# ScalarE's exponentials placed ahead of the sinks' copy and of the values' copy in an attention kernel with a written-out order

## The chip, the cores and the metric

One core of a Trainium2 chip runs one program. The core has five engines with a queue each, worked in order: TensorE (PE in the profile; its weight loads are PEld), VectorE (DVE), ScalarE (ACT), GpSimd (POOL) and SyncE (SP, which here issues the DMAs). An engine waits on semaphores for what the others produce. Times are device microseconds (us) of one execution; the metric is the median over runs.

## The reference

Two parts, one after the other. Attention for batch 4, 8 heads, 768 positions, head size 64: each query sees the first 4 keys (the sinks) and the 128 latest keys up to itself. Then a mixing layer and a feed-forward layer on the 512 columns that the heads make together:

```python
keep = is_sink | in_window                     # n_sink = 4, window = 128
scores = np.where(keep, scale * q @ k.T, -1e9)
a = np.exp(scores - np.max(scores, axis=-1, keepdims=True))
x = (a / (np.sum(a, axis=-1, keepdims=True) + 1e-09)) @ v
...
u = x + np.real(np.fft.fft(np.fft.fft(x, axis=1), axis=2))
un = (u - mean(u)) / np.sqrt(var(u) + 1e-06)
out = u + np.maximum(un @ w_ch1, 0.0) @ w_ch2  # 512 -> 2048 -> 512
```

All is float32.

## The kernel before

**Blocks and steps.** The attention goes over 24 blocks: 4 batches of 6 blocks of 128 queries. A block has 4 steps, one for each pair of heads. So step s works on block g = s // 4 and pair s % 4, called here the first to the fourth step of a block (k = 0 to 3). Every operation of a pair or a block is issued a fixed number of steps after its scores: `STEP_LAG` for what is done per pair, `BLOCK_AT` for what is done per block. A step therefore holds the scores of one pair, the exponentials of the pair two steps earlier, the transposes of an earlier one, and so on.

**One pair, in order.** PE makes the scores (L700, L702) in a PSUM tile `s`, of which there are two. DVE merges the older key block into the place of the masked newer keys (`merge`, L708) and subtracts the maximum with the mask (`soft1`, L720) into the tile `sm`. ACT takes the exponentials of the two heads, one ACTIVATE each, with their sums (`expo`, L726, two steps after the scores). POOL copies the sinks' four columns aside as a rounded part and a remainder (`sink_p`, L737 and L738). PE transposes the probabilities of four heads (`trans_p`, L751), ACT copies them out of PSUM (`copy_p`, L758, tile `pta`), POOL splits them into newer and older keys (L767, L775), and PE multiplies by the values (`av`, L789) into `xt`.

**One block.** PE transposes the sinks' probabilities (`trans_sink`, L809); the result lies in a part of the score tile of the second pair two blocks later, so the merge into that tile comes after ACT has copied it out (`copy_sink`, L814, tile `skt`, always in a block's second step). ACT copies the values' product `xt` out of PSUM (`copy_x`, L794, tile `xs`, always in a fourth step). PE turns it and adds the sinks' part (`turn_x`, L801, L803), and DVE scales it into the residual (`store_x`, L819).

**The Fourier mix** of a batch starts when its blocks are stored, and runs as events between the steps of the next batch: folds on DVE and POOL (L351, L358, L361), a rounded copy on ACT (`gh`, L364) and its remainder on DVE (`gl`, L367), products on PE (L394, L421, L442), their copies on ACT (L399, L401, L425, L430) and remainders or sums on DVE (L406, L409, L447, L448), updates on POOL (L458, L459). On ACT these copies are the entry `"A"` of an order. They free the PSUM bank that PE's next product takes.

**What sets the order.** In steps 0 to 96 each engine's instructions are issued exactly in the order that the table `SCHEDULE` writes out: a row for each of the four steps of a block, for each of the four engines A (ACT), V (DVE), G (POOL), T (PE). The table has two sets of rows: the first for steps below `PHASE = 36`, the second from there on. An entry with nothing to do in a step (as `sink_hi` outside the first step, or `copy_p` in the first and third) issues nothing. From step `CUT = 97` on the framework's planner places the instructions, by costs that it assumes, up to the end of the first group of the feed-forward layer. The weights' conversions (`convert`, L590 to L592 on DVE, L607 on ACT, L608 on POOL) belong to it. Then come the other groups of the feed-forward layer (L619, L1124 on PE), again in written order.

Of the kernel before, what the change touches and what calls it, by code (L numbers as in the profile page):

```python
# [83 lines left out]
    {  # L84
        "A": [
            ["copy_x", "copy_p", "copy_sink", "expo", "A", "sink_hi"],
            ["copy_x", "copy_sink", "expo", "sink_hi", "A", "copy_p"],
            ["copy_x", "copy_p", "copy_sink", "expo", "A", "sink_hi"],
            ["copy_x", "A", "copy_p", "copy_sink", "expo", "sink_hi"],
        ],  # L90
        "V": [
            ["inverse", "store_x", "sink_lo", "V", 3, 0, 1, 2, "merge", "soft1"],
# [17 lines left out]
    {  # L110
        "A": [
            ["copy_x", "copy_p", "A", "sink_hi", "copy_sink", "expo"],
            ["copy_x", "copy_sink", "A", "sink_hi", "copy_p", "expo"],
            ["copy_x", "copy_p", "copy_sink", "expo", "A", "sink_hi"],
            ["expo", "copy_x", "copy_p", "copy_sink", "A", "sink_hi"],
        ],
# [1220 lines left out]
```

## Time and profile before

| | us |
|---|---|
| median of 3 runs | 787.84 (786.68 to 789.1) |
| the profiled execution | 786.78 |
| its span | 784.9 |
| PE busy in it | 755.2 |
| DVE busy | 460.6 |
| ACT busy | 239.0 |
| POOL busy | 177.6 |
| last exponential of the attention starts | 205.5 |

The profile gives for each group of instructions the line, the engine, the operation, the tiles (out<-in), their number and time, and the idle time of the engine just ahead of them with the instruction that ended it. In a listing in order of time, the columns are start, duration, engine, line, operation, tiles, shapes and count; idle time stands in brackets behind.

### The profile page before, as it was taken

Reading aid. Unit: us, or ns where it says so; the run is one execution under the profiler, and the core shown is the slowest. Engines: PE = TensorE matmul, PEld = TensorE weight load, DVE = VectorE, ACT = ScalarE, POOL = GpSimd, SP = SyncE. Lnnn points to the kernel's source line nnn. Section 1 sums busy time; section 2 is a strip of 40 time slices with the busy share of each in tenths; the row PEclk is TensorE's granted clock in tenths of the full one; section 3 lists DMA queues with packets and bytes.
Section 4 is the critical chain, followed back from the end, with each engine's and each line's share of the span. In section 5 each row is a group of like instructions: output and inputs, shape, how many; then the busy total and the mean of one; then the engine's idle time right before and its main releaser. Section 6 shows DMA issues by size and latency. Waiting matters only on the chain.

```text
span 784.9 us, 11953 instructions
## 1 busy us (share of the span) xinstructions
PE 755.2 (96%) x4379; PEld 615.8 (78%) x4379; DVE 460.6 (59%) x1354; ACT 239.0 (30%) x704; POOL 177.6 (23%) x283
## 2 busy tenths in 40 slices
PE   7999998988899999999999999999999999999996
PEld 5666876866778878899888888888888888888895
DVE  6788687999999589561356424662456425611211
ACT  4887765756633133221111111111111110110110
POOL 2566477476645255200000000000000000000000
PEclk9999999999999999999999999999999999999999
DMA  9853525433305366120100002000200001000100
GB/s 311 251 171 109 140 84 176 127 112 99 131 27 159 111 196 210 62 71 1 54 1 0 1 9 99 1 1 0 81 1 0 1 0 54 1 1 0 55 1 32
DMA packets 41812, 57.69 MB, mean 74 GB/s; under 512 B 2796, under 2 KB 27500, under 8 KB 41360
## 3 DMA queue, kind: packets, MB, share of 16 engines
q1 hardware_dynamic: 41456, 53.07, 21.7%
q0 software_dynamic: 288, 3.76, 1.2%
q8 instruction: 37, 0.61, 0.3%
q14 instruction: 31, 0.25, 0.1%
HBM read 47.37 MB, written 9.45 MB: 72 GB/s over the span
## 4 chain that ended last, share of the span: by engine, by line
PE 80%; DVE 13%; issue 2%; POOL 1%; ACT 1%; DMA 1%; SPq 0%; DVEq 0%; ACTq 0%; POOLq 0%
PE h L619 33%; PE o L1124 33%; PE xt L789 3%; PE s L702 3%; DVE sm L720 2%; PE pt L751 2%; DVE cv L591 1%; PE za L394 1%; DVE s L708 1%; DVE cv L590 1%; PE a L421 1%; DVE cv L592 1%; DVE f L351 1%; PE x L801 1%; DMA vt<-in_v_sink_dram 1%
## 5 line engine op out<-in xcount | busy, mean ns | idle before, releaser
L1124 PE MATMUL o<-w,h 128*128 128x512 f32 x876 | 216.5, 394 | 0.0
L1117 DVE SCALAR_TENSOR_TENSOR h<-h,h 128x512 fp32r<-128x512 f32 (+1 forms) x107 | 65.4, 611 | 247.7 <-ACT h L1112 247.5
L1124 PEld LDWEIGHTS o<-w,h 128*128 128x128 f32 x876 | 162.8, 188 | 35.5
L1112 ACT ACTIVATE h<-h 128x512 fp32r<-128x512 f32 (+1 forms) x107 | 57.2, 535 | 366.4 <-PE h L619 360.1
L619 PE MATMUL h<-un_slots,w 128*128 128x512 f32 (+1 forms) x576 | 124.7, 365 | 0.0
L619 PEld LDWEIGHTS h<-un_slots,w 128*128 128x128 f32 x576 | 99.6, 188 | 19.6
L619 PE MATMUL h<-un_last,w 128*128 128x512 f32 (+1 forms) x432 | 89.0, 355 | 0.0
L619 PEld LDWEIGHTS h<-un_last,w 128*128 128x128 f32 x432 | 72.7, 188 | 12.8
L726 ACT ACTIVATE sm<-sm,mx 128x132 f32<-128x132 f32 x192 | 75.8, 400 | 7.1 <-DVE mx L720 7.1
L1148 DVE STREAM_TRANSPOSE unf<-un 32x128 f32<-32x128 f32 x224 | 67.7, 302 | 3.2
L702 PE MATMUL s<-ring,q 64*128 64x260 f32 x320 | 51.2, 422 | 12.2 <-DVE mx L720 6.4
L720 DVE CUSTOM_DVE_ANT_0 sm<-s,mask 128x132 f32<-128x132 f32 x192 | 48.7, 292 | 9.3 <-ACT skt L814 2.7
L702 PEld LDWEIGHTS s<-ring,q 64*128 64x128 f32 x320 | 27.1, 188 | 28.2 <-issue 12.4
L608 POOL TENSOR_TENSOR w<-cv,w 128x512 fp32r<-128x512 f32 x25 | 33.9, 1354 | 35.5 <-ACT w L607 35.4
L789 PE MATMUL xt<-ptl,ldv 128*64 128x128 f32 x384 | 38.9, 288 | 0.0
L708 DVE COPY_PREDICATED s<-older,s 128x256 f32<-128x256 uint8 x80 | 33.6, 420 | 7.2 <-ACT skt L814 6.8
L726 ACT ACTIVATION_READ_ACCUMULATOR sm<-sm,mx 128x1 f32 x192 | 36.8, 192 | 0.0
L1124 PE MATMUL o<-w_ring,h 128*128 128x512 f32 x144 | 35.6, 393 | 0.0
L767 POOL TENSOR_SCALAR_AFFINE_SELECT ptl<-pta 128x512 f32<-128x512 f32 x48 | 32.2, 672 | 14.4 <-ACT pta L758 14.4
L789 PEld LDWEIGHTS xt<-ptl,ldv 128*64 128x64 f32 x384 | 21.6, 137 | 14.9 <-issue 8.1
L789 PE MATMUL xt<-pta,ldv 128*64 128x128 f32 x320 | 31.7, 277 | 0.2 <-POOL pta L775 0.2
L751 PE MATMUL pt<-ident,sm 128*128 128x128 f32 x192 | 31.6, 288 | 0.0
(200 smaller groups left out, 1040.9 us busy)
## 6 DMA issues: line engine op xcount, KB each, us to landing
raw<-in_moe_w_ch_dram SPq DMA_DIRECT2D x32, 512.0 KB, 3.7
ldv<-in_v_dram SPq DMA_DIRECT2D x28, 256.0 KB, 3.6
ring<-in_qk_dram SPq DMA_DIRECT2D x24, 264.0 KB, 4.6
out_dram<-u SPq DMA_DIRECT2D x24, 256.0 KB, 3.8
q<-in_qk_dram SPq DMA_DIRECT2D x20, 256.0 KB, 4.2
cst<-in_dft_dram POOLq DMA_DIRECT2D x1, 3348.0 KB, 11.7
ud<-us SPq DMA_DIRECT2D x12, 256.0 KB, 2.2
u<-ud SPq DMA_DIRECT2D x2, 1024.0 KB, 5.1
```

What stands on the lines that cost most here:

```text
L608: G.tensor_tensor(d[1], tf, f32(d[0]), op=ALU.subtract)
L619: T.matmul(ps[:, :tb], a[:, cs], x[:, :, cc, :], start=n == 0, stop=n == 3 * NCC - 1)
L702: T.matmul(ps[:, j, :P + W], st["q", g][rows, hp, :], keys(g, 2 * hp + j), start=True, stop=True)
L708: V.copy_predicated(ps[:, :, P + NS:P + W], older[qi > 2], ps[:, :, 0:P])
L720: V.tensor_tensor_reduce(sm[:, h % 4], ps[:, j, P:P + W], mask[min(qi, 3)], -SCALE, 3.0e38, ALU.add, ALU.min, accum_out=mx[:, 0, h:h + 1])
L726: A.activation(sm[:, h % 4], sm[:, h % 4], AF.Exp, bias=mx[:, 0, h:h + 1], scale=-1.0, accum_out=mx[:, 1, h:h + 1])
L751: T.transpose(ps[:, j], sm[:, j, NS:], ident)
L789: T.matmul(ps[D * j:D * j + D, p, :], st["v", kb(g) - i][:, h, :], a[:, h % 4, :], start=i == 0, stop=i == n - 1)
L1112: A.activation(h[0], ps[:, :tb], AF.Relu)
L1117: V.scalar_tensor_tensor(h[1], ps[:, :tb], 0.0, f32(h[0]), op0=ALU.max, op1=ALU.subtract)
L1124: T.matmul(po[i], a[:, ts_], x, start=f == 0 and n == 0, stop=f == NF - 1 and n == 2)
L1148: V.transpose(unf[32 * q:32 * q + 32, :, r], un[r].rearrange("p (c q j) -> p c q j", c=NCC, q=4)[:, :, q])
```

## The change

Three rows of the order of ACT are written differently; no instruction is added or taken away.

```diff
 SCHEDULE = [
     {
         "A": [
             ["copy_x", "copy_p", "copy_sink", "expo", "A", "sink_hi"],
-            ["copy_x", "copy_sink", "expo", "sink_hi", "A", "copy_p"],
+            ["copy_x", "expo", "copy_sink", "copy_p", "A", "sink_hi"],
             ["copy_x", "copy_p", "copy_sink", "expo", "A", "sink_hi"],
-            ["copy_x", "A", "copy_p", "copy_sink", "expo", "sink_hi"],
+            ["expo", "copy_x", "A", "copy_p", "copy_sink", "sink_hi"],
         ],
...
     {
         "A": [
             ["copy_x", "copy_p", "A", "sink_hi", "copy_sink", "expo"],
-            ["copy_x", "copy_sink", "A", "sink_hi", "copy_p", "expo"],
+            ["copy_x", "expo", "copy_sink", "copy_p", "A", "sink_hi"],
             ["copy_x", "copy_p", "copy_sink", "expo", "A", "sink_hi"],
             ["expo", "copy_x", "copy_p", "copy_sink", "A", "sink_hi"],
         ],
```

In the second step of a block the exponentials go ahead of the sinks' copy, in both sets of rows, and the Fourier copies (`"A"`) go behind the probabilities' copy. In the fourth step of the first set the exponentials go ahead of the values' copy; the second set had that order already. The second step's exponentials are those of the fourth pair of the block before; the fourth step's are those of the second pair of its own block.

## The prediction

> **What bounds the kernel now.** I read the page first, then busy time by stretch, then the groups of instructions, last the single queues in order of time.
>
> ```profile
> PE 755.2 (96%) x4379; PEld 615.8 (78%) x4379; DVE 460.6 (59%) x1354; ACT 239.0 (30%) x704; POOL 177.6 (23%) x283
> ```
>
> ScalarE (ACT), the only engine whose order is edited, is busy 30% of the span. The edited steps end near 208 us, so what counts is that part, by stretch (columns: length, then busy time with the count of instructions of PE, weight loads, DVE, ACT, POOL, then the granted clock, DMA share, GB/s):
>
> ```profile
> 17.00:57.00 40.00, 39.14 (x374) 27.62 (x375) 32.40 (x167) 32.98 (x132) 22.18 (x51) 0.97 0.73 233
> 57.00:72.00 15.00, 13.17 (x118) 8.67 (x117) 13.89 (x58) 11.35 (x45) 12.53 (x22) 1.00 0.36 110
> 72.00:105.00 33.00, 33.00 (x297) 27.65 (x296) 21.59 (x94) 22.46 (x84) 15.19 (x33) 1.00 0.42 114
> 105.00:122.00 17.00, 13.01 (x108) 9.12 (x107) 15.73 (x48) 11.30 (x43) 14.11 (x22) 0.98 0.28 80
> 159.00:186.00 27.00, 20.95 (x180) 15.48 (x180) 26.45 (x84) 15.74 (x54) 20.85 (x34) 1.00 0.38 113
> 200.00:256.00 56.00, 52.14 (x324) 44.31 (x321) 55.51 (x96) 22.34 (x52) 32.44 (x30) 0.97 0.32 102
> ```
>
> Two kinds alternate. In 17 to 57 and 72 to 105 us PE has 0.86 and 0 us idle: it is the bound, and a wait moved on ACT, DVE or POOL changes nothing. In 57 to 72, 105 to 122, 159 to 186 and 200 to 256 us DVE is 93 to 99% busy and PE idles 1.8, 4.0, 6.1 and 3.9 us. There only what shortens DVE's own queue helps. ACT binds no stretch.
>
> Who waits around the edit, from the groups (after the bar: busy us and mean ns of one, then idle time before and its releasers):
>
> ```profile
> L726 ACT ACTIVATE sm<-sm,mx 128x132 f32<-128x132 f32 x192 | 75.8, 400 | 7.1 <-DVE mx L720 7.1
> L708 DVE COPY_PREDICATED s<-older,s 128x256 f32<-128x256 uint8 x80 | 33.6, 420 | 7.2 <-ACT skt L814 6.8 <-PE s L702 0.5
> L794 ACT COPY xs<-xt 128x512 f32<-128x512 f32 x24 | 14.1, 586 | 16.7 <-PE xt L789 16.2 <-PE x L801 0.5
> L737 POOL CAST sk<-sm 128x32 fp32r<-128x32 f32 x48 | 11.3, 236 | 58.9 <-ACT sm L726 58.7
> ```
>
> The exponentials wait only 7.1 us for their input, so they can mostly run where they are put; behind one that did wait would stand skt and pta, and behind skt DVE's merge. The values' copy (xs) waits 16.2 us for PE. POOL loses 58.7 us waiting for exponentials. And DVE's merge waits 6.8 us for the sinks' copy (skt), because the transposed sinks lie in the score buffer that this merge writes: what delays skt delays DVE.
>
> **The change, part by part.** Nothing is added or removed; no DMA is issued from these lines.
>
> *What is put ahead.* One pair of exponentials takes 0.79 us of ACT's queue (32.14 to 32.93):
>
> ```profile
> 31.98 0.27 ACT L814 CAST skt<-s 128x128 fp32r<-128x128 f32 x1
> 32.14 0.41 ACT L726 ACTIVATE sm<-sm,mx 128x132 f32<-128x132 f32 x1
> 32.93 0.57 ACT L758 COPY pta<-pt 128x512 f32<-128x512 f32 x1
> 33.40 0.41 ACT L726 ACTIVATE sm<-sm,mx 128x132 f32<-128x132 f32 x1
> ...
> 35.27 0.59 ACT L794 COPY xs<-xt 128x512 f32<-128x512 f32 x1 [0.99 <-PE xt L789]
> ...
> 47.51 0.59 ACT L794 COPY xs<-xt 128x512 f32<-128x512 f32 x1 [0.28 <-PE xt L789]
> ```
>
> *First order (steps below 36).* skt at 31.98 has no idle ahead of it, so alone the move would delay DVE by 0.79 us a block. But the fourth step gives one pair away: it now runs ahead of the values' copy. From that copy to the next skt there are four exponentials before (pairs of the second and third scores) and four after (third and fourth). So skt keeps its place wherever the copy of the values keeps its own. That copy has 0.99 us of idle at 35.27, enough for 0.79; at 47.51 it has 0.28, so it and the next skt come 0.51 late. PE is the bound there (39.14 of 40.00): I cost it 0, and up to 0.5 if that cover fails.
>
> *Second order.* The pair simply goes ahead of skt. The shortest idle of ACT there is 0.54 us:
>
> ```profile
> 90.79 0.27 ACT L814 CAST skt<-s 128x128 fp32r<-128x128 f32 x1 [0.54 <-PE s L809]
> ...
> 155.37 0.36 ACT L425 COPY dcs<-dc 1x257 f32<-1x257 f32 x1
> ...
> 175.85 0.38 ACT L430 COPY asb<-a 128x257 f32<-128x257 f32 x1 [0.19 <-PE a L421]
> ```
>
> At 90.79 skt comes 0.25 late, under a PE without idle: 0. The probabilities' copy (pta) now goes ahead of the Fourier copies. It holds ACT for 0.47 us (32.93 to 33.40). Where a Fourier copy sits ahead of it with a shorter wait, that copy comes late and with it PE's next Fourier product, which waits for the freed bank: up to 0.47 at 155.37 (no idle marked) and 0.28 at 175.85 (0.47 less the 0.19). Between 0 and 0.75 I take the middle, **+0.4 us**, since in both places DVE may be later still.
>
> *What gets earlier.* With the pair done before skt, POOL's wait for it goes. At 105 to 122 us this reaches DVE:
>
> ```profile
> 111.81 0.21 POOL L737 CAST sk<-sm 128x32 fp32r<-128x32 f32 x1 [2.15 <-ACT sm L726]
> ...
> 116.10 0.82 POOL L767 TENSOR_SCALAR_AFFINE_SELECT ptl<-pta 128x512 f32<-128x512 f32 x1
> 116.90 1.70 POOL L351 TENSOR_TENSOR f<-us,us 128x512 f32<-128x512 f32 x1
> ```
> ```profile
> 113.81 0.59 ACT L758 COPY pta<-pt 128x512 f32<-128x512 f32 x1
> ```
> ```profile
> L351 DVE TENSOR_TENSOR f<-us,us x9: 639/693/1758, 95.8 to 228.6; 128x512 f32<-128x512 f32 x9
> 117.39 1.76 DVE L351 TENSOR_TENSOR f<-us,us 128x512 f32<-128x512 f32 x1
> ```
>
> DVE's fold at 117.39 takes 1.76 us against a median of 0.69 because POOL's fold runs beside it. POOL's queue can move by 2.15 at the first wait and, held by pta (done 114.40), by 1.70 at 116.10; its fold then ends about 116.5, before DVE's begins: **-1.07 us** on DVE. [...]
>
> The same at the smaller folds, whose median is 0.42:
>
> ```profile
> L361 DVE TENSOR_TENSOR f<-f x12: 405/420/897, 51.5 to 229.2; 128x255 f32<-128x255 f32 x12
> 58.27 0.86 DVE L361 TENSOR_TENSOR f<-f 128x255 f32<-128x255 f32 x1
> 62.86 0.21 POOL L737 CAST sk<-sm 128x32 fp32r<-128x32 f32 x1 [1.39 <-ACT sm L726]
> 63.54 0.74 DVE L351 TENSOR_TENSOR f<-u 128x512 f32<-128x512 f32 x1
> 64.74 1.27 POOL L351 TENSOR_TENSOR f<-u 128x512 f32<-128x512 f32 x1
> 65.98 0.90 DVE L361 TENSOR_TENSOR f<-f 128x255 f32<-128x255 f32 x1
> 178.90 0.85 DVE L361 TENSOR_TENSOR f<-f 128x255 f32<-128x255 f32 x1
> ```
>
> The three at 58.27, 65.98 and 178.90 run beside POOL work that I let move by 1.39 to 2.15 us, the two waits shown: -0.44, -0.48, -0.43. But POOL's fold at 64.74, freed of the 1.39 us wait at 62.86, moves to about 63.3, onto DVE's fold at 63.54, now 0.74: +1.07, the price of that meeting at 117.39. Where each meeting ends is unknown; bounds are -1.35 (no new one) and +1.07 (none avoided). I take the sum, -0.28, as POOL's queue gives it.
>
> **Sum:** -1.07 - 0.28 + 0.40 = -0.95 us. The profiled execution took 786.78 us (1.88 of it outside its span of 784.9, both in the table above), 1.06 below the median 787.84 of runs from 786.68 to 789.1; it goes to 785.8, the median to **786.9 us**. Bounds: -1.07 - 1.35 = -2.4, and +1.07 + 0.75 + 0.5 = +2.3.
>
> **The rivals.** *The clock comes back too (faster).* After DVE's late fold PE waits 2.31 us and then runs at half clock:
>
> ```profile
> 120.19 0.71 PE L702 MATMUL s<-ring,q 64*128 64x260 f32 x4 [2.31 <-DVE mx L720]
> 106.75 1.15 PE L702 MATMUL s<-ring,q 64*128 64x260 f32 x8 [1.15 <-DVE d L448]
> ```
> ```profile
> 106.75:109.00 2.25, 2.25 (x22) 1.74 (x22) 2.25 (x2) 0.36 (x2) 2.25 (x3) 1.00 0.30 116
> 122.00:124.90 2.90, 2.90 (x21) 2.26 (x20) 1.88 (x12) 0.59 (x1) 2.75 (x7) 0.51 0.00 0
> ```
>
> 2.90 us at 0.51 would take 1.48 at full clock, so 1.42 more could go; a wait of 1.15 us was followed by 1.00. With it, no new meeting and no late copy: -1.07 - 1.35 - 1.42 = -3.84, **784.0**. For it: the wait falls to 1.24. Against: DVE is busy for 15.73 of the 17 us to 122, so a faster PE may only wait for it. [...]
>
> *POOL lands on DVE's folds (slower).* At 63.54 us, if POOL's fold starts before DVE's: +1.07, the late Fourier copies 0.4, and if PE's wait there passes the 2 us, half clock for 1.42; nothing avoided elsewhere: +2.9, **790.7**. For it: DVE is 93% busy there. Against: PE's waits in that stretch now add up to 1.8 us, so no single one is near the 2.31 that was followed by half clock. The point from which it decides is a POOL fold that starts before 63.54. [...]
>
> *The end is laid out anew.* From step 97 the framework's planner, not the written order, places the instructions, weight conversions among them. It sees other ACT times. A conversion that sits before a Fourier remainder costs now:
>
> ```profile
> 206.64 2.41 DVE L591 SCALAR_TENSOR_TENSOR cv<-raw,cv 128x512 int32<-128x512 int32 x2
> 209.57 0.62 PE L394 MATMUL zb<-cst,gh 128*128 128x386 f32 x2 [2.05 <-DVE zb L409]
> 210.00:212.00 2.00, 2.00 (x10) 1.90 (x9) 2.00 (x7) 0.62 (x1) 0.65 (x2) 0.54 0.17 20
> ```
>
> 2.05 of wait and 2.00 x 0.46 = 0.92 of clock: about 3 us either way, **785 or 791**.
>
> *Nothing moves*: POOL is held by other inputs, the exponentials only change their place: **787.8**.
>
> **Chances.** Forecast 0.40, nothing moves 0.12, clock too 0.29, POOL's landing 0.12, planner 0.07 (0.03 faster, 0.04 slower). What a measurement can tell from no change is 0.3%, 2.4 us: below 785.5 counts as faster, above 790.2 as slower. Faster 0.29 + 0.03 = 0.32, same 0.52, slower 0.16. The forecast's own range is its bounds, 785.4 to 790.1; to leave out no more than 2 in 10 it reaches to 783.4, a little below the clock case, and to 790.2, short of the landing.
>
> **What would show it.** Right: POOL's waits for exponentials fall from 58.7 us by about a third; skt's wait for PE shrinks by some 0.8 us a block while DVE's wait for skt stays near 6.8; no DVE fold of 1.76 us near 117. Wrong: DVE's wait for skt grows by several us in the first order (the swap isn't neutral); new folds over 1 us on DVE; half clock at a new place; PE's idle between 57 and 186 us grows; another order of conversions after 178 us.

## The result, and the profile after

The changed kernel takes 791.87 us (791.18 to 792.21), the kernel before beside it 787.84 (786.66 to 789.1): a ratio of 1.0055, with a 95% interval of 1.0043 to 1.0067. It is slower by 4 us, where 786.9 was forecast and 790.2 was the end of the range.

From the page of the changed kernel, PE's busy time hardly differs (755.2 before), so nearly all of the 5.1 us by which its span of 790.0 exceeds 784.9 are waits of PE. DVE's and POOL's busy times are 3.2 and 2.7 us longer for the same instructions (460.6 and 177.6 before):

```profile
PE 755.8 (96%) x4379; PEld 616.8 (78%) x4379; DVE 463.8 (59%) x1354; ACT 239.7 (30%) x704; POOL 180.3 (23%) x283
```

Two of the groups that the prediction showed, after the change (busy us and mean ns of one, then idle time ahead of them and what ended it):

```profile
L708 DVE COPY_PREDICATED s<-older,s 128x256 f32<-128x256 uint8 x80 | 33.7, 421 | 8.8 <-ACT skt L814 6.5 <-PE s L702 2.3
...
L737 POOL CAST sk<-sm 128x32 fp32r<-128x32 f32 x48 | 13.5, 282 | 27.3 <-ACT sm L726 27.2
```

The change does what it says. POOL's wait for exponentials fell from 58.7 to 27.2 us, and DVE waits for skt no longer than before (6.5 against 6.8). But POOL's next input, the probabilities' copy, is now what it waits for: its masks' wait for pta (L767) rose from 14.4 to 42.0 us. POOL as a whole waits about as long as before, at other places in its queue. The time went elsewhere. Busy time by stretch, with the columns of before:

```profile
17.00:57.00 40.00, 35.66 (x353) 25.73 (x351) 31.20 (x157) 30.67 (x122) 21.88 (x48) 1.00 0.69 208
57.00:72.00 15.00, 10.97 (x88) 6.85 (x88) 14.52 (x50) 10.48 (x41) 11.04 (x17) 1.00 0.36 102
72.00:105.00 33.00, 33.00 (x304) 27.23 (x303) 20.65 (x97) 22.75 (x82) 14.95 (x33) 1.00 0.47 133
```

PE idles 4.34 us in 17 to 57 (before 0.86, with half clock up to about 19 us, 0.50 granted at 17 to 19, counted as busy) and 4.03 in 57 to 72 (before 1.83); from 72 on it is full again. To find the places, I took the start of the sinks' copy (skt) of each block in the listing of ACT, and its difference to before:

| block | 0 | 1 | 2 | 3 | 4 | 5 | 6 | 7 | 8 | 12 | 14 | 23 |
|---|---|---|---|---|---|---|---|---|---|---|---|---|
| before, us | 19.97 | 25.69 | 31.98 | 38.50 | 44.93 | 50.34 | 57.10 | 64.53 | 71.94 | 109.17 | 127.76 | 215.38 |
| after, difference | -0.66 | +1.11 | +0.96 | +1.81 | +1.82 | +2.45 | +2.34 | +3.59 | +4.69 | +5.11 | +4.94 | +4.72 |

The whole loss arises before 77 us, in steps: 1.77 between blocks 0 and 1, 0.85 between 2 and 3, 0.63 between 4 and 5, 2.35 between 6 and 8. The second order, from step 36 on, adds nothing. Each step has its rows in the listing in order of time. First the start, and block 4:

```profile
8.91 0.71 POOL L294 DMA_DIRECT2D cst<-in_dft_dram  x1
...
24.38 1.15 PE L702 MATMUL s<-ring,q 64*128 64x260 f32 x8 [1.75 <-DMA ring<-in_qk_dram]
...
50.37 1.15 PE L702 MATMUL s<-ring,q 64*128 64x260 f32 x8 [0.57 <-DMA ring<-in_qk_dram]
```

PE waits 1.75 and 0.57 us for keys of the ring, which it does nowhere in the trace of before. The load of the Fourier constants (3.3 MB) is not issued by SyncE but by POOL, from its own queue, behind its first sinks' copy. That copy waits for exponentials, so the load now starts at 8.91 us; before it was this row:

```profile
11.87 0.71 POOL L294 DMA_DIRECT2D cst<-in_dft_dram  x1
```

Block 2, before and then after:

```profile
33.18 0.21 DVE L926 TENSOR_SCALAR scratch<-scratch 32x4 f32<-32x4 f32 x1
33.43 0.26 DVE L927 TENSOR_SCALAR scratch<-scratch 32x64 f32<-32x64 f32 x1
33.59 0.64 POOL L767 TENSOR_SCALAR_AFFINE_SELECT ptl<-pta 128x512 f32<-128x512 f32 x1
```
```profile
34.11 0.64 POOL L767 TENSOR_SCALAR_AFFINE_SELECT ptl<-pta 128x512 f32<-128x512 f32 x1 [0.50 <-ACT pta L758]
34.13 0.63 DVE L926 TENSOR_SCALAR scratch<-scratch 32x4 f32<-32x4 f32 x1
34.80 0.69 DVE L927 TENSOR_SCALAR scratch<-scratch 32x64 f32<-32x64 f32 x1
34.81 0.64 POOL L775 TENSOR_SCALAR_AFFINE_SELECT pta<-pta 128x512 f32<-128x512 f32 x1
```

POOL's two masks now run beside two small instructions of DVE (the first query's row), which take 1.32 us in place of 0.47. DVE is 0.85 us late, and the block is 0.85 us late.

Blocks 6 and 7, before and then after:

```profile
55.79 0.69 DVE L351 TENSOR_TENSOR f<-u 128x512 f32<-128x512 f32 x1
57.58 1.27 POOL L351 TENSOR_TENSOR f<-u 128x512 f32<-128x512 f32 x1
...
62.48 0.42 DVE L377 TENSOR_TENSOR sph<-xr,sph 1x257 fp32r<-1x257 f32 x1
62.93 0.69 DVE L367 TENSOR_TENSOR gl<-f,gh 128x512 fp32r<-128x512 f32 x1
```

```profile
57.75 0.64 POOL L767 TENSOR_SCALAR_AFFINE_SELECT ptl<-pta 128x512 f32<-128x512 f32 x1 [1.38 <-ACT pta L758]
57.99 0.94 DVE L367 TENSOR_TENSOR gl<-f,gh 128x512 fp32r<-128x512 f32 x1
58.35 1.71 POOL L351 TENSOR_TENSOR f<-u 128x512 f32<-128x512 f32 x1
58.85 1.76 DVE L351 TENSOR_TENSOR f<-u 128x512 f32<-128x512 f32 x1
...
61.65 0.71 PE L702 MATMUL s<-ring,q 64*128 64x260 f32 x4 [1.11 <-DVE mx L720]
62.31 0.42 DVE L361 TENSOR_TENSOR f<-f 128x255 f32<-128x255 f32 x1
...
66.21 1.31 POOL L351 TENSOR_TENSOR f<-u 128x512 f32<-128x512 f32 x1
66.42 1.38 DVE L377 TENSOR_TENSOR sph<-xr,sph 1x257 fp32r<-1x257 f32 x1
67.47 0.82 POOL L775 TENSOR_SCALAR_AFFINE_SELECT pta<-pta 128x512 f32<-128x512 f32 x1
67.83 1.01 DVE L367 TENSOR_TENSOR gl<-f,gh 128x512 fp32r<-128x512 f32 x1
...
70.49 0.71 PE L702 MATMUL s<-ring,q 64*128 64x260 f32 x4 [1.75 <-DVE mx L720]
71.16 0.42 DVE L361 TENSOR_TENSOR f<-f 128x255 f32<-128x255 f32 x1
```

POOL's fold starts at 58.35, half a microsecond ahead of DVE's, where it came 1.79 us behind it before; DVE's takes 1.76 us. In block 7 POOL's next fold, and the mask behind it, run beside the small row update (L377) and gl. PE waits 1.11 and 1.75 us for DVE behind them.

DVE's own queue accounts for the step of these blocks. From 54 to 74 us, and over the same instructions before (51.5 to 69.5 us), DVE waits for nothing and has the same order, so it can only fall behind by instructions that take longer. Against before it is 2.44 us late at 53.98 and 4.70 at 74.19. The steps between are +0.43 (a small fold and a row copy ahead of 56 us), +0.25 and +1.08 (gl and the fold at 58 us), +0.36, +0.96 and +0.32 (L375, L377 and gl at 65.8 to 68.8), and -0.45 and -0.49: the folds at 62.31 and 71.16, 0.86 and 0.90 before, take 0.42 as predicted. Everything else adds up to -0.2. Each of the instructions that grew runs beside one of POOL.

### The profile page after: what moved, and what is told of

Read it like the earlier page. It is cut to its first block, busy times and chain, and to the rows that moved or that the text cites. A ratio compares the mean times of both kernels' runs of the same rounds, so it can differ in the third digit from the quotient of the medians.

```text
span 790.0 us, 11962 instructions
## 1 busy us (share of the span) xinstructions
PE 755.8 (96%) x4379; PEld 616.8 (78%) x4379; DVE 463.8 (59%) x1354; ACT 239.7 (30%) x704; POOL 180.3 (23%) x283
## 4 chain that ended last, share of the span: by engine, by line
PE 77%; DVE 15%; DMA 3%; issue 2%; SPq 1%; ACT 1%; POOL 1%; DVEq 0%; ACTq 0%; POOLq 0%
PE h L619 32%; PE o L1124 32%; PE xt L789 3%; PE s L702 3%; DMA ring<-in_qk_dram 3%; DVE sm L720 2%; DVE cv L591 1%; PE za L394 1%; DVE s L708 1%; PE pt L751 1%; DVE f L351 1%; DVE cv L590 1%; DVE cv L592 1%; DVE gl L367 1%; PE a L421 1%
## 5 line engine op out<-in xcount | busy, mean ns | idle before, releaser
L767 POOL TENSOR_SCALAR_AFFINE_SELECT ptl<-pta 128x512 f32<-128x512 f32 x48 | 31.0, 646 | 42.2 <-ACT pta L758 42.0
L758 ACT COPY pta<-pt 128x512 f32<-128x512 f32 x48 | 28.2, 587 | 12.1 <-PE pt L751 12.0
```

Source lines behind the costliest of these rows:

```text
L767: G.affine_select(lo, a, [[0, 4], [s, P]], compare_op=ALU.is_ge, fill=0.0, base=0, channel_multiplier=-s)
```

## Experiments: which rows

The theories, as the expectations name them: L, the one formed from the trace above (an early load and POOL beside DVE); F, the Fourier copies behind pta; S, skt and pta late behind the exponentials. The first four runs (the three that follow here without the fourth row alone, and the first on the constants) left of L only that POOL's early work meets DVE's: theory P, with the rivals E (the folds cost nothing, blocks pass on an earlier loss) and M (POOL meets some instruction of DVE wherever it goes).

All comparisons are with the kernel before, run beside on the same chip. A kernel that keeps some rows of before has this in place of the plain lookup; only the last condition differs from one to the next:

```diff
-                                for op in SCHEDULE[s >= PHASE][e][k]:
+                                for op in row(s, e, k):
...
+def row(s, e, k):
+    o = int(s >= PHASE)
+    if e == "A" and (o, k) in BEFORE_ROWS and (o == 1):
+        return BEFORE_ROWS[o, k]
+    return SCHEDULE[o][e][k]
```

In the four kernels whose edit stands in the first part of the file (the first three here, and the first on the constants) lines are 14 higher: L828 is L814, L365 is L351.

**The first order alone** (condition as above).

> Only the two rows of the first order are new, the second order's row is that of before. Theory L (the loss arises before 77 us: the constants' load, issued from POOL's queue, starts 3 us earlier and delays the keys, +1.8 and +0.6; POOL and DVE run beside each other in blocks 2, 6 and 7, +0.85, +1.25, +1.1; the rest near zero): the whole loss is here, 791.4 to 792.3. Rival F (the Fourier copies behind pta in the second order cost it): 787.4 to 788.4. Rival S (skt and pta behind the exponentials make DVE's merge late in every block with the new second row, 24 of them): some 3/10 of the loss, for 7 of the 24 blocks, about 789.

791.64 us against 786.53, ratio 1.0068 (1.0051 to 1.0084). The whole loss is in the first order's two rows.

**The second order alone.**

```diff
+    if e == "A" and (o, k) in BEFORE_ROWS and (o == 0):
```

> Only the second order's row (steps from 36) is new. Theory L: 787.3 to 788.4, the same as before. Rival F: most of the loss, 790.5 to 792. Rival S: 17 of 24 blocks, some 7/10 of the loss, about 790.7.

787.02 against 786.53, ratio 1.0008 (0.9998 to 1.0017): no difference. This run also tests the prediction's largest gain, the DVE fold of 1.76 us at 117 us, since its trace is like that of before up to there (columns as in the listing, lines 14 higher):

```profile
111.22 0.85 DVE L385 TENSOR_TENSOR xr<-xr 33x255 f32<-33x255 f32 x1
115.16 1.28 POOL L365 TENSOR_TENSOR f<-us,us 128x512 f32<-128x512 f32 x1
115.47 1.12 DVE L389 CAST sph<-xr 33x257 fp32r<-33x257 f32 x1
...
118.33 1.21 DVE L365 TENSOR_TENSOR f<-us,us 128x512 f32<-128x512 f32 x1
120.58 0.71 PE L716 MATMUL s<-ring,q 64*128 64x260 f32 x4 [2.15 <-DVE mx L734]
```
```profile
111.12 0.41 DVE L371 TENSOR_TENSOR xr<-xr 33x255 f32<-33x255 f32 x1
115.00 0.65 DVE L375 CAST sph<-xr 33x257 fp32r<-33x257 f32 x1
```

The second fence is the kernel before. POOL's fold moved from 116.90 to 115.16, by 1.74 us (1.70 was predicted), and DVE's fold went from 1.76 to 1.21. But an earlier POOL runs beside DVE's two row instructions, its mask at 110.91 beside the first and the fold beside the second, and they went from 0.41 and 0.65 to 0.85 and 1.12. That is +0.91 against -0.55, and PE still waits 2.15 us there.

**The second row of the first order alone** (the exponentials ahead of skt, nothing given back in the fourth step).

```diff
+    if e == "A" and (o, k) in BEFORE_ROWS and (o == 1 or k == 3):
```

> Only the second row of the first order is new, so that the exponentials go ahead of skt and nothing is given back in the fourth row: skt comes up to 0.79 us later in each of 7 blocks, and the constants' load stays where it was. Theory L: constants not early (no +2.4), PE still bound in 17 to 57 us, so at most the collisions of POOL and DVE: 787.8 to 790. Rival S: 7 times up to 0.79 us, 790.5 to 793.4, and DVE's wait for skt grows from 6.8 us by several.

790.26 against 786.53, ratio 1.0042 (1.0026 to 1.0058). DVE's wait for skt is now

```profile
L722 DVE COPY_PREDICATED s<-older,s 128x256 f32<-128x256 uint8 x80 | 33.6, 420 | 9.6 <-ACT skt L828 9.0 <-PE s L716 0.5
```

9.0 in place of 6.8 at the merge, and 3.5 in place of 2.7 at the soft maximum: +3.0 us, and the blocks fall behind by 0.3 to 0.8 us each from 1 to 6 (in the table below). Rival S is right for this row alone; theory L, which had at most the collisions, fell here. With both rows new this wait is back at 6.5, so it isn't how the changed kernel loses.

**The fourth row alone.**

```diff
+    if e == "A" and (o, k) in BEFORE_ROWS and (o == 1 or k == 1):
```

> Only the fourth row of the first order is new: the exponentials go ahead of the values' copy, and the next skt comes up to 0.79 us earlier. Theory P: the start-up as in the changed kernel (+0.5 to +1.1) and POOL early enough to meet DVE's folds (+2.3): +2.5 to +4 us against before. Theory of the giving back (what the second row alone loses, 0.5 to 0.7 us a block, this row wins): -3 to -1. If neither: within 1 us of before.

790.45 against 787.22, ratio 1.0037 (1.0022 to 1.0052). Nothing is won where PE is the bound, so the theory of the giving back falls, and the loss between blocks 6 and 8 is there: 3.08 us. A half clock at 70 to 74 us (0.51 and 0.64 granted) is part of that; the changed kernel's trace has none there (1.00). So each row loses alone, by another way, and the two together lose by the second of them.

## Experiments: which steps

**New rows in steps 0 to 7 only** (the rows of before from step 8, in the second order too).

```diff
+    if e == "A" and (o, k) in BEFORE_ROWS and (s >= 8):
```

> The new rows in steps 0 to 7 only, the rows of before from step 8. The early constants' load alone is left of the change. If the losses come place by place, as the changed kernel's trace has them: the start-up's +0.8 to +1.1 us (PE waits for keys near 24 us), none in block 2 to 3 and none at POOL's folds: +0.5 to +1.2 us against before. If the start-up's delay goes on growing later by itself: +2 or more.

787.14 against 787.04, ratio 1.0004 (0.9995 to 1.0013). In the profiled execution PE waits for keys here too, 1.07 us at 23.66, and block 8 is 1.04 us late; by block 14 it is 0.51 early, because no half clock follows the wait of 2.16 us at 121.11 (1.00 granted at 122 to 130) as it did in the kernel before at 120.19 (0.51 at 122 to 124.9). I had expected +0.5 to +1.2. The early load is real in the trace and worth nothing that the median shows.

**Rows of before in steps 8 to 27.**

```diff
+    if e == "A" and (o, k) in BEFORE_ROWS and (8 <= s < 28):
```

> The changed kernel with the rows of before in steps 8 to 27: new in steps 0 to 7 (+0.4 measured alone), in 28 to 35 and in the second order. Theory P: the loss in block 2 (+0.85) goes, that of the folds stays: +2.3 to +3.5 against before. If the steps 8 to 27 prepare POOL's lead, which the folds then need: +0.5 to +1.5, and no DVE fold of 1.76 us near 58.

791.59 against 787.84, ratio 1.0045 (1.0028 to 1.0062). The 0.85 us between blocks 2 and 3 are gone (2.80 and 2.80 late), and 3.69 us are lost between blocks 6 and 8, so POOL's lead of the last two blocks is enough. DVE's stretched rows are those of the changed kernel, which lost 2.35 there; in this trace half clock follows (0.52 and 0.62 at 72 to 76 us), which goes with the rest.

**Rows of before in steps 28 to 35.**

```diff
+    if e == "A" and (o, k) in BEFORE_ROWS and (28 <= s < 36):
```

> The changed kernel with the rows of before in steps 28 to 35 only, the last two blocks of the first order, where POOL's folds run on DVE's (58 to 71 us). Theory P (these meetings cost 2.3 to 2.6 us of the loss): against before +2.2 to +3.0 us instead of +4 to +5, and no DVE fold of 1.76 us before 72 us. Rival E (the blocks only pass on what was lost before them, the folds cost nothing by themselves): +4 to +5, as the changed kernel.

788.72 against 787.22, ratio 1.0027 (1.0011 to 1.0043), so about 2.2 us come back (0.0055 less 0.0027 of 787), with an uncertainty of some 1.6 us. DVE's and POOL's folds stand apart again:

```profile
56.98 0.68 DVE L351 TENSOR_TENSOR f<-u 128x512 f32<-128x512 f32 x1
...
58.63 1.27 POOL L351 TENSOR_TENSOR f<-u 128x512 f32<-128x512 f32 x1
```

and blocks 6, 7 and 8 are 1.05 us late, all three alike. Theory P holds and rival E falls. By medians the changed kernel's 0.0055 is then 0.0028 for steps 28 to 35 (this run), 0.0010 for 8 to 27 (the run before it), 0.0004 for 0 to 7 and 0.0008 for the second order, each with an uncertainty of about 0.001 to 0.002; the sum is 0.0050. Only the first of the four is clear of zero.

## Experiments: the constants' load

**The first block's fourth step as before**, so that POOL's first sinks' copy and the load are late again (12.68 us in its trace).

```diff
+    if e == "A" and (o, k) in BEFORE_ROWS and (s == 3):
```

> The changed kernel with the fourth row of before in one step only, the first block's (step 3): the first sinks' halves go ahead of the exponentials again, so POOL's sink copy and with it the constants' load should be back at about 11.9 us. Theory L: PE's waits of 1.75 us at 22.6 and 0.6 us at 49.8 for the keys go, the collisions stay: 791.87 - 2.4 = 789.5. If the load's start is not what delays the keys: 791.9, and PE still waits for the ring of keys near 22.6 us.

790.99 against 786.53, ratio 1.0054 (1.0036 to 1.0071): not the 2.4 us hoped for. The wait for keys at 22 to 24 us is gone, but PE waits 2.28 us for DVE ahead of 14.87 and then runs at half clock to 22 us (mean granted clock of its profiled run 0.992, of the changed kernel's 0.994), as before it did to 19 (0.50 at 17 to 19). The start is lost in one way or the other. The wait near 50 us stays (0.53 us), so the early start of the load is not what causes that one; its cause is open.

**The load in step 10, in the changed kernel and in the one before.**

```diff
-                                        if (s, op) == (4, "G"):
+                                        if (s, op) == (10, "G"):
```

> The changed kernel with the constants' load and POOL's two fills in step 10 instead of step 4, about 27 us, after the keys of the first blocks. If the early load delays the keys: PE's waits of 1.75 us near 22.6 and 0.6 near 49.8 for the ring of keys go, -1.8 to -2.4 against the changed kernel, so +2 to +3 against before. If the load isn't what delays them: no change, +4 to +5.

> The kernel before with the constants' load and POOL's two fills in step 10 instead of step 4. The fills no longer run beside DVE's 0.82 us instruction near 11.1 us (0.25 alone): DVE comes 0.57 us earlier, PE's wait of 1.90 us near 14 falls to about 1.3 and the half clock behind it (15 to 19 us, about 2 us lost) may go: -0.6 to -2.6 us against before. If start-up is set by the loads of queries and keys: 0.

The changed kernel with this takes 790.12 against 787.22, ratio 1.0034 (1.0019 to 1.0049); the kernel before 788.35, ratio 1.0023 (1.001 to 1.0036). In the first PE no longer waits for keys and block 1 is 0.39 early in place of 1.11 late, so in this trace the load's place is worth 1.5 us to the start. In the second the load starts at 22.83 us and PE waits for the next keys instead, 1.69 us here and 1.15 at 50.72:

```profile
37.66 1.15 PE L702 MATMUL s<-ring,q 64*128 64x260 f32 x8 [1.69 <-DMA ring<-in_qk_dram]
```

DVE's instruction near 11 us did shorten (0.82 to 0.23 us), but the wait ahead of 14 us did not (2.05, before 1.90): POOL's fills were not its cause, as I had supposed.

**The load in step 26**, where the transfers leave a gap: with new rows in steps 0 to 7 only, and in the kernel before.

```diff
-                                        if (s, op) == (4, "G"):
+                                        if (s, op) == (26, "G"):
```

> As the run with the new rows in steps 0 to 7 only, and the constants' load with POOL's two fills moved from step 4 to step 26 (about 46 us), where the transfers leave a gap (0.10 and 0.00 of the DMA engines at 46 to 52 us, the constants are first read at 71.7). If the load is what delays the keys: no wait for the ring of keys, -0.5 to -1.5 us against before, since the half clock of 15 to 19 us goes too. If it isn't: +0.5 to +1.2.

> The kernel before with the constants' load and POOL's two fills in step 26 instead of step 4; its order is that of before. If a load that meets the keys costs them about 1.7 us, as at step 10: no wait for the ring now, -0.5 to +0.3 us against before. If any later place costs as at step 10: +1 to +2.4.

787.35 (ratio 1.0003, 0.9992 to 1.0013) and 787.37 (1.0009, 1.0 to 1.0018) against 787.04. No wait for keys is left in either trace, and neither is faster, though -0.5 to -1.5 us was expected of the first. In the kernel before, step 10 costs something clear of noise (0.10 to 0.36%), step 26 hardly (0.00 to 0.18%).

## Experiments: POOL's fold

**POOL's first fold one step later** than DVE's, in the changed kernel.

```diff
-F_N, F_M, F_S, ROW = (3, 3), (4, 5), (6, 7), (5, 8, 10)
+F_N, F_M, F_S, ROW = (3, 4), (4, 5), (6, 7), (5, 8, 10)
```

> The changed kernel with POOL's first fold of each pair one step later than DVE's (all batches but the last). If the loss at 58 to 71 us comes from POOL's folds starting before DVE's: those DVE folds are back at about 0.7 us and +2 to +3 us against before instead of +4 to +5. If POOL only meets other instructions of DVE then: +4 to +5, with other DVE rows stretched.

790.99 against 787.04, ratio 1.0057 (1.0042 to 1.0072): nothing gained. POOL's fold still meets DVE's. In the trace its queue near 57 us has the order that it has in the changed kernel (mask, fold, sinks' copy), so the edit moved nothing there:

```profile
56.82 1.12 DVE L351 TENSOR_TENSOR f<-u 128x512 f32<-128x512 f32 x1
...
57.37 1.70 POOL L351 TENSOR_TENSOR f<-u 128x512 f32<-128x512 f32 x1
```

**POOL's fold at the end of its step**, in the changed kernel and in the one before (this row in both orders).

```diff
-            ["newer_p", "G", "older_p", "sink_p"],
+            ["newer_p", "older_p", "sink_p", "G"],
```

> The changed kernel with POOL's event (its first fold) moved in each block's first step, in both orders, from its second place to its last, behind the masks of both probabilities and the sinks' copy. Theory P (POOL's fold starts before DVE's and stretches it): the folds near 58 and 67 us start behind DVE's, those DVE folds take 0.7 to 0.75 us, and the loss falls to +1.5 to +3 us against before. Rival M (POOL's work meets some DVE instruction wherever it goes): +4 to +5, with other DVE rows over 0.8 us.

> The kernel before with POOL's first fold at the same later place. Theory P: nothing at 57.6 and 64.7 us, where DVE's folds are not stretched, and the DVE fold of 1.76 near 117 us goes back to 0.7: -2.4 (with the half clock behind it) to 0. Rival M: 0 to +2.

The changed kernel with this: 791.98 against 787.84, ratio 1.005 (1.0032 to 1.0068). The fold it was meant for did not move against its neighbours, because the step at 58 us has no second mask and its sinks' copy belongs to the next step. The one that did move met gl:

```profile
59.01 1.71 POOL L351 TENSOR_TENSOR f<-u 128x512 f32<-128x512 f32 x1
59.51 1.76 DVE L351 TENSOR_TENSOR f<-u 128x512 f32<-128x512 f32 x1
...
67.58 1.44 POOL L351 TENSOR_TENSOR f<-u 128x512 f32<-128x512 f32 x1
67.91 1.65 DVE L367 TENSOR_TENSOR gl<-f,gh 128x512 fp32r<-128x512 f32 x1
```

That speaks for rival M, which belongs beside P: in these rows POOL's folds lie on DVE's fold and on gl, which take 1.76 and 1.65 us where they took 0.69 each in the kernel before (at 55.79 and 62.93).

The kernel before with it: 786.52 against 787.84, ratio 0.9986 (0.9975 to 0.9998): at most a little faster, since the interval ends at 0.02% and this is one of fifteen such comparisons. The meeting at 117 us is milder there, by ordering POOL and not ACT:

```profile
120.11 1.12 DVE L351 TENSOR_TENSOR f<-us,us 128x512 f32<-128x512 f32 x1
122.27 0.71 PE L702 MATMUL s<-ring,q 64*128 64x260 f32 x4 [0.96 <-DVE mx L720]
122.39 1.27 POOL L351 TENSOR_TENSOR f<-us,us 128x512 f32<-128x512 f32 x1
```

DVE's fold takes 1.12 in place of 1.76, and PE waits 0.96 us in place of 2.31. Its profiled execution was the longest of its twelve, so its differences by block are no measure of a gain, and no trace shows one.

The start of skt in the profiled execution of the runs on rows and steps, and of one on the load, as a difference to before in us, by block:

| | 1 | 2 | 3 | 6 | 8 | 12 | 14 | 23 |
|---|---|---|---|---|---|---|---|---|
| after | +1.11 | +0.96 | +1.81 | +2.34 | +4.69 | +5.11 | +4.94 | +4.72 |
| first order | +0.55 | +0.39 | +1.24 | +1.11 | +3.73 | +3.72 | +3.24 | +4.80 |
| second order | +0.11 | +0.11 | +0.10 | +0.10 | +0.09 | +0.08 | +0.31 | +0.18 |
| second row alone | +1.65 | +2.18 | +2.75 | +4.41 | +4.19 | +4.04 | +3.71 | +3.65 |
| fourth row alone | +1.07 | +1.07 | +1.06 | +1.67 | +4.75 | +4.61 | +4.13 | +3.97 |
| new in 0 to 7 | +0.39 | +0.39 | +0.39 | +0.79 | +1.04 | +0.92 | -0.51 | -0.60 |
| old in 8 to 27 | +2.81 | +2.80 | +2.80 | +3.20 | +6.89 | +7.24 | +6.11 | +5.95 |
| old in 28 to 35 | +0.78 | +0.62 | +1.46 | +1.05 | +1.05 | +2.08 | +0.97 | +0.69 |
| after, load in step 10 | -0.39 | -0.54 | +0.30 | +0.68 | +4.45 | +4.35 | +4.49 | +4.36 |

## Why the prediction was wrong

**The swap is neutral on ACT: right.** With both rows new DVE waits for skt 6.5 us, before 6.8; with the second row alone 9.0. The fourth row gives back what the second takes, as the count of exponentials said.

**The second order: no gain came.** It was taken as -1.07 at 117 us, -0.43 at 179 and +0.40 for Fourier copies behind pta, -1.10 in all; alone it measures +0.6 (-0.2 to +1.3). The Fourier copies cost about nothing: the copy at 155.37 us started at 156.36, but skt ahead of it was 0.76 late already, and behind the one at 175.85 the scores are no later than ahead of it. What made skt late, up to 0.95 (block 18), was mainly POOL again: at 147.91 and 148.76 two small DVE instructions took 0.62 and 0.48 in place of 0.16 us beside its masks. All but 0.17 of it was made good by block 20, where the fold that took 0.85 at 178.90 takes 0.42, as predicted. At 117 us POOL moved as worked out, but its mask and its fold met two other instructions of DVE.

**"PE is the bound there: I cost it 0": wrong.** In 17 to 57 us PE had 0.86 us idle in 40, which I read as room for everything else. It says nothing about how late a single product comes when DVE is stretched ahead of it. Block 2 lost 0.85 us that way, and about 0.8 us by the medians, though that is not clear of noise.

**"What gets earlier": the step that failed.** It moved POOL by the two waits whose rows I had picked (1.39 and 2.15) and looked only at DVE's folds. In 17 to 72 us POOL's wait for exponentials fell from 20.0 to 3.0 us, but 15.0 us for pta and 2.4 for DVE took its place (who waited for what: us in total, times, longest; before and after):

```profile
POOL sk L737 <- ACT sm L726: 20.0, 11, 3.9
```
```profile
POOL ptl L767 <- ACT pta L758: 15.0, 13, 2.5
POOL sk L737 <- ACT sm L726: 3.0, 8, 1.1
POOL f L358 <- DVE f L361: 2.4, 3, 1.2
```

So POOL did not run freely ahead. Its queue stopped at other places, and its folds and masks came to lie beside other instructions of DVE than before. The term for 57 to 72 us stood at -0.28 with +1.07 as its worst; the runs show about +2.2 for steps 28 to 35 (the medians with and without them). The two small folds that were to get shorter there did, by -0.45 and -0.49. Left out were the meetings with gl, L375 and L377, +0.25 to +0.96 each, and the fold's +1.07 was met in full (+1.08) one block earlier than it was placed.

**The landing, a rival with a chance of 0.12, is nearest to what happened.** It named a POOL fold ahead of DVE's, placed it at 63.54 us and priced the kernel at 790.7. The fold landed one earlier, at 58.35, and in the next block on L377 and gl. "No single wait is near the 2.31", the argument against it, held for the waits of before: they became 1.11 and 1.75. No half clock followed in the changed kernel's trace (1.00 granted at 70 to 76 us), so the price was made of DVE's stretched rows instead; that 790.7 lies near the 791.87 measured is in part luck. In other kernels with these meetings half clock did follow, between 70 and 78 us: 0.51 granted at 70 to 72 us with the fourth row alone, 0.52 at 72 to 74 with rows of before in 8 to 27. The 2 us from which the rival reckoned with it was an estimate of mine that fits three waits of the kernel before (1.15 us followed by 1.00, 2.05 by 0.54, 2.31 by 0.51), and the runs do not bear it out: 1.64 us was followed by half clock and 2.47 was not (last section).

**A DMA that moved: missed.** I wrote that these lines issue none. POOL's queue does, behind the sinks' copy that a moved exponential releases, and the load moved by 2.96 us. PE waits 1.75 us for keys in the trace of the changed kernel, and between none and 2.12 us in the traces of the seven other kernels whose load starts near 8.8 us; with new rows in steps 0 to 7 only, the median stays within 0.13% of before. The forecast lost nothing measurable by it, but it was luck.

**The planner: excluded.** The order of the instructions of PE, DVE, POOL and SyncE is the same in both kernels, and the difference of skt stays between 4.72 and 4.80 from block 20 on.

**What stays open.** That the meetings make DVE late in blocks 6 to 8 is shown by its queue, which waits for nothing there, and steps 28 to 35 are shown to hold about half of the loss. All kernels here that have POOL's fold of 1.7 us on DVE's near 58 us lose over 1.5 us between blocks 6 and 8, and those that have it behind DVE's lose at most 0.4. No run moved POOL's fold alone out of DVE's way there: both edits that were to do so left POOL's order at that place as it was. How much of the median loss is half clock, which follows the meetings in some traces and not in others, is open. Whether steps 0 to 7 cost nothing, or 1 us that other executions win back elsewhere as the profiled one did, is not settled either.

## What to carry to other kernels

Before an engine is made faster, list what its queue will do earlier, DMA issues among them, and put every instruction of it against what the neighbour that it was seen to stretch does at that moment, not only against the like instruction that met it so far. A wait that goes may only move to the next input, as POOL's went from the exponentials (58.7 to 27.2 us) to pta (14.4 to 42.0). A stretch in which one engine is nearly full, as PE here with 39.14 of 40.00 us, is no cover for a delay on another that feeds it: block 2 lost 0.85 us there. Where two engines meet, it may be better to order the one that does the meeting: moving POOL's fold in the kernel before gained 0.14% (0.02 to 0.25%, barely clear of noise), moving ACT's exponentials to free POOL lost 0.55%.

## What the hardware showed

In these traces a half clock did not follow from the length of a wait alone. Granted clock behind three waits of PE, from busy time by stretch (the clock is the third number from the end), in the changed kernel behind 2.45 us at 125.60, in the kernel with rows of before in 28 to 35 behind 2.47 us at 122.58, and in that with the fourth row alone behind 1.64 us at 69.14:

```profile
126.00:128.00 2.00, 2.00 (x12) 0.98 (x12) 1.86 (x10) 1.05 (x6) 1.41 (x5) 0.50 0.00 0
```
```profile
124.00:126.00 2.00, 2.00 (x24) 1.55 (x24) 1.82 (x10) 0.72 (x3) 1.92 (x5) 1.00 0.00 0
```
```profile
70.00:72.00 2.00, 1.97 (x12) 1.33 (x14) 1.85 (x6) 0.59 (x4) 1.42 (x4) 0.51 0.00 0
```

So 1.64 us was followed by half clock and 2.47 was not. At one and the same place, behind the meetings of block 7, 1.75 us was not followed by it in the changed kernel (1.00 at 70 to 76 us) and 1.73 us was in the kernel with rows of before in 8 to 27 (0.52 at 72 to 74). A threshold of length alone near 2 us, as the prediction used it, does not hold in these rows; what besides the length decides no run here shows.

Single-input instructions of DVE were stretched beside POOL too: L926 from 0.21 to 0.63 us, and the cast at L375 from 0.23 alone to 0.59 in the changed kernel and 1.12 with the second order alone. I had looked for that at the two-input folds alone.
